# One batch of attention: the product of probabilities and values in plain fp32 instead of hi and lo parts

## The chip, the cores and the metric

The kernel runs on one core of a Trainium2 chip. The metric is the device time of one execution in microseconds (us). A core has a matrix engine (TensorE, PE in the rows; its weight loads are listed apart as PEld), VectorE (DVE), ScalarE (ACT), GpSimd (POOL) and SyncE (SP), which here only issues DMA transfers. Each engine works off its own instructions in their order.

## What is computed

```python
# q, k, v: (4 batches, 12 heads, 448 positions, 64)
q_n, k_n = rmsnorm(q, g_q), rmsnorm(k, g_k)
scores = (q_n @ k_n.T) / sqrt(64)
attn = exp(scores - scores.max(-1)); attn = attn / (attn.sum(-1) + 1e-9)
x = (attn @ v)                       # heads side by side: (1792, 768)
x = relu(x @ w_in)**2 @ w_out        # 768 -> 2048 -> 768
x = ((x @ w1) * (x @ w2)) @ w3 @ w_out2   # 768 -> 1024 -> 1024 -> 768
```

The heads' outputs are gathered to 768 columns and go through two dense blocks. All is fp32 to the caller; the weights arrive as 64-bit numbers.

## The kernel before, in words

**Exact products from rounded parts.** A matmul on tiles of type fp32r rounds its operands. To keep the bits, an operand is written as two fp32r tiles: hi, a rounded copy, and lo, what is left of it (`sub_on`, line 114). A dense product is then three matmuls (lines 262 to 264: hi times hi, hi times lo, lo times hi). ScalarE mostly makes hi (`copy_on`, line 106), GpSimd and VectorE make lo. A weight tile (a "unit", `raw` and `hl` in the rows) goes through a load on SP's queue (line 180), a conversion from 64 bits on ScalarE and GpSimd (lines 194 to 200), a join on VectorE (line 207) and the split.

**Stages.** While the 12 heads of the first batch go through attention, the free slots of TensorE are filled with the product w3 @ w_out2 (`gen_w3o`, 384 matmuls of 384 columns). While the heads of a later batch do so, the dense blocks of the batch before are the filling (`gen_moe`); the last batch's blocks end the kernel. `fill(n)` puts n matmuls of the filling at six places of each head's iteration.

**A head** (loop over `h`, two iterations deep). Scores in two halves of two row chunks each (`stage_qk`, lines 524 to 527: matmuls `sc<-kt,qh` and `sc<-kt,ql`, then the maximum on VectorE), the exponentials on ScalarE (`stage_exp`, line 543, tile `p`), one iteration later the transposes of `p` (`stage_t`, line 570: for each of four key chunks `kc` four transposes into one PSUM tile `pt`), and the product with the values (`stage_v`, line 622: `kv<-ptr,vhl`). The scores have two PSUM tiles, so the next two chunks of scores wait for the exponentials of the last two. Before the change a transposed chunk leaves PSUM twice: ScalarE copies hi, VectorE subtracts lo. The fourth chunk has 64 keys; its hi and lo lie one above the other in one tile (`pte`), so the product is seven matmuls of 448 columns, on weights `vhl` that hold the hi and lo parts of the values side by side (`v_prep`: a copy on VectorE, a subtraction on GpSimd in this batch). Its result has two halves, which ScalarE (tile `vt`) and VectorE (line 630) add up into `xf`. Every second head the row sums (`rsw`) are transposed (line 611) and multiplied in (line 636).

**Order.** The code above is the priority only. A scheduler of the framework sets the order of each engine's instructions from the dependences and its own idea of durations, and hands buffers of a pool to tiles as they come free.

**SP's queue** takes loads and stores in one order. A load whose buffer is not free holds up all that stand behind it. The value tile `v` has two buffers.

Of the kernel before, what the change touches and what calls it, by code (L numbers as in the profile page):

```python
# [8 lines left out]
F32 = mybir.dt.float32  # L9
# [20 lines left out]
def attention_moe_kernel(  # L30
# [15 lines left out]
    nc = tc.nc  # L46
    B, P, H, C, D = q_nat.shape
    S = P * C
# [10 lines left out]
    KCS = ((0, 128), (128, 128), (256, 128), (384, 64))  # L59
# [27 lines left out]
    t2 = ctx.enter_context(tc.tile_pool(name="t2", bufs=2))  # L87
    t1 = ctx.enter_context(tc.tile_pool(name="t1", bufs=1))
    t3 = ctx.enter_context(tc.tile_pool(name="t3", bufs=3))
# [4 lines left out]
    ps_kv = ctx.enter_context(tc.tile_pool(name="ps_kv", bufs=1, space=bass.MemoryType.PSUM))  # L94
# [9 lines left out]
    def copy_on(eng, out, in_):  # L104
        if eng == "a":
            nc.scalar.activation(out=out, in_=in_, func=AF.Copy)  # L106
        elif eng == "g":
            nc.gpsimd.tensor_scalar(out=out, in0=in_, scalar1=1.0, scalar2=1.0, op0=ALU.mult, op1=ALU.mult)
        else:
            nc.vector.tensor_copy(out=out, in_=in_)  # L110

    def sub_on(eng, out, in0, in1):
        e = nc.vector if eng == "v" else nc.gpsimd
        e.tensor_tensor(out=out, in0=in0, in1=in1, op=ALU.subtract)  # L114
# [273 lines left out]
    heads = {}  # L388
# [173 lines left out]
    def stage_t(h, kc):  # L562
        if not (0 <= h < NH):
            return
        d = heads[h]
        k0, kn = KCS[kc]
        ps = ps_pt.tile([128, 512], F32, name="pt", tag="pt")
        to, one = (ps.bitcast(F32R), ident_r) if h >= H else (ps, ident)
        for c in range(C):
            nc.tensor.transpose(to[:kn, c * P:(c + 1) * P], d["p"][c][:, k0:k0 + kn], one)  # L570
        if kn == 128:
            t = t3.tile([128, 2, S], F32R, name="ptr", tag="ptr", bufs=3)
            hi, lo = t[:, 0, :], t[:, 1, :]
            d["pt"][kc] = [hi, lo]
        else:
            t = t1.tile([128, S], F32R, name="pte", tag="pte")
            hi, lo = t[:kn, :], t[kn:, :]
            d["pt"][kc] = [t]
        copy_on("a", hi, ps[:kn, :S])
        d["lo"].append((lo, ps[:kn, :S], hi.bitcast(F32)))  # L580
# [9 lines left out]
    def v_prep(h):  # L590
        if not (0 <= h < NH):
            return
        v = vs.pop(h)
        t = t2.tile([128, C, 2, D], F32R, name="vhl", tag="vhl")
        i = h % 2
        copy_on("v", t[:, :, i, :], v)
        sub_on(VLO_ENG[h // H], t[:, :, 1 - i, :], v, t[:, :, i, :].bitcast(F32))
        heads[h]["v"] = t

    xf = {}  # L600
# [13 lines left out]
    def stage_v(h):  # L614
        if not (0 <= h < NH):
            return
        d = heads.pop(h)
        vt = d["v"].rearrange("p c a d -> p c (a d)")
        ps = ps_kv.tile([128, 512], F32, name="kv", tag="kv")
        ops = [(vt[:, kc, :], m) for kc in range(4) for m in d["pt"][kc]]  # L620
        for n, (w, m) in enumerate(ops):
            nc.tensor.matmul(ps[:, :S], w, m, start=(n == 0), stop=(n == len(ops) - 1))  # L622
        i = h % 2
        r0, r1 = i * D, (1 - i) * D
        if i == 0:
            xf[0] = t2.tile([128, S], F32, name="xf", tag="xf")
        x = xf[0]
        tmp = t1.tile([128, S], F32, name="vt", tag="vt")
        copy_on("a", tmp[r0:r0 + D, :], ps[r1:r1 + D, :S])
        nc.vector.tensor_tensor(out=x[r0:r0 + D, :], in0=ps[r0:r0 + D, :S], in1=tmp[r0:r0 + D, :], op=ALU.add)  # L630
# [45 lines left out]
    for h in range(NH + 1):  # L676
# [8 lines left out]
        if h % H != 1:  # L685
            stage_x(h - 2)
        stage_t(h - 1, 0)
        stage_t(h - 1, 1)
        fill(n)
        stage_lo(h - 1)  # L690
        if h < NH:
            v_prep(h)
        fill(n)
        stage_k(h + 1)
        stage_t(h - 1, 2)
        stage_t(h - 1, 3)
        fill(n)
# [3 lines left out]
        stage_exp(h, 1)  # L701
        fill(n)
        stage_v(h - 1)
        if h % GH == 1:
            group_prep(h // GH + 1)
# [62 lines left out]
```

## Time and profile before

| | |
|---|---|
| median of 3 runs | 1241.29 us (1238.86 to 1243.09) |
| profiled execution, its own time | 1239.56 us |
| span of its trace | 1237.8 us |
| TensorE busy | 1166.3 us, 94% of the span |
| VectorE, ScalarE, GpSimd busy | 57%, 59%, 63% |
| granted TensorE clock, mean | 0.986 |

Shares over the whole span mix stages with different limits, so the rows below go by stretches. In a timeline a row is one or several instructions: start, time from the start of the first to the end of the last, engine, line, operation, tiles, and in brackets the idle time of the engine ahead of it with what ended it. A matmul's listed duration holds its latency: the next one starts while it drains, so the cost of a matmul in a stream is the distance from start to start.

### The profile page before, as it was taken

How to read it: one execution, taken by the hardware profiler on the slowest of the kernel's cores; microseconds unless marked ns; L12 is line 12 of the kernel's file. 1: busy time of each engine (PE TensorE's matmuls, PEld its weight loads, DVE VectorE, ACT ScalarE, POOL GpSimd, SP SyncE). 2: the span in 40 equal slices, each digit the busy share in tenths (PEclk: the TensorE clock that was granted, in tenths of full speed). 3: DMA queues.
4: the chain of work that ended last, by engine and by line, in shares of the span. 5: the costliest groups of instructions: out<-in, count | busy, mean ns of one | idle time of the engine just before them, and what ended most of it. 6: DMA issues, size and time to landing. Idle time of an engine off the chain costs nothing.

```text
span 1237.8 us, 18914 instructions
## 1 busy us (share of the span) xinstructions
PE 1166.3 (94%) x6192; PEld 1054.4 (85%) x6192; DVE 710.7 (57%) x1314; ACT 727.7 (59%) x1553; POOL 784.9 (63%) x772
## 2 busy tenths in 40 slices
PE   3799999898898999999999999999999999999998
PEld 1588887787787888998998998999999999999998
DVE  6699888878888685546567555655664421012110
ACT  5888867667746655655645655656545554443342
POOL 5875434565776756765776664756766556678673
PEclk9899999999999999999999999999999999999999
DMA  6774547787888866455445455454444443433342
GB/s 214 242 227 131 159 140 218 254 272 249 280 259 257 257 192 194 132 155 147 148 127 154 140 155 161 143 154 121 141 138 120 135 136 112 113 109 105 105 120 93
DMA packets 111347, 207.63 MB, mean 168 GB/s; under 512 B 12208, under 2 KB 66704, under 8 KB 111248
## 3 DMA queue, kind: packets, MB, share of 16 engines
q1 hardware_dynamic: 107792, 200.92, 53.8%
q10 hardware_dynamic: 3456, 5.51, 1.2%
q8 instruction: 49, 0.80, 0.3%
q14 instruction: 50, 0.41, 0.1%
HBM read 149.95 MB, written 27.53 MB: 143 GB/s over the span
## 4 chain that ended last, share of the span: by engine, by line
PE 59%; DMA 4%; DVE 4%; ACT 2%; POOL 1%; issue 1%; ACTq 0%; SPq 0%; POOLq 0%; DVEq 0%
PE mm L262 17%; PE mm L264 17%; PE mm L263 17%; PE kv L622 3%; PE pt L570 2%; DMA pw<-p 2%; PE sc L525 1%; PE sc L524 1%; DMA raw<-w 1%; POOL hl L114 1%; ACT p L543 1%; DMA kn<-k_nat 1%; PE kv L508 1%; DVE nb L526 1%; DVE raw L207 0%
## 5 line engine op out<-in xcount | busy, mean ns | idle before, releaser
L114 POOL TENSOR_TENSOR hl<-raw,hl 128x384 fp32r<-128x384 f32 (+1 forms) x383 | 447.0, 1171 | 254.5 <-ACT hl L106 250.9
L106 ACT ACTIVATE hl<-raw 128x384 fp32r<-128x384 f32 (+1 forms) x416 | 233.8, 564 | 146.8 <-PE mm L264 82.0
L262 PE MATMUL mm<-x,hl 128*128 128x448 f32 (+1 forms) x832 | 311.3, 374 | 4.4 <-ACT x L106 1.8
L263 PE MATMUL mm<-x,hl 128*128 128x448 f32 (+1 forms) x832 | 307.2, 369 | 8.1 <-POOL x L114 8.1
L264 PE MATMUL mm<-x,hl 128*128 128x448 f32 (+1 forms) x832 | 306.4, 368 | 3.7 <-DVE hl L114 3.3
L262 PE MATMUL mm<-act,hl 128*128 128x448 f32 (+1 forms) x640 | 238.3, 372 | 0.0
L263 PE MATMUL mm<-act,hl 128*128 128x448 f32 (+1 forms) x640 | 235.7, 368 | 2.3 <-POOL act L114 2.3
L264 PE MATMUL mm<-act,hl 128*128 128x448 f32 (+1 forms) x640 | 235.0, 367 | 0.6 <-POOL hl L114 0.6
L543 ACT ACTIVATE p<-sc,nb,rr 112x448 f32<-112x448 f32 x192 | 137.4, 720 | 82.4 <-DVE nb L527 82.0
L263 PEld LDWEIGHTS mm<-x,hl 128*128 128x128 f32 x832 | 158.5, 190 | 21.9 <-POOL x L114 9.7
L262 PEld LDWEIGHTS mm<-x,hl 128*128 128x128 f32 x832 | 158.4, 190 | 19.6 <-ACT x L106 3.5
L264 PEld LDWEIGHTS mm<-x,hl 128*128 128x128 f32 x832 | 158.6, 191 | 18.3 <-DVE hl L114 4.0
L526 DVE TENSOR_REDUCE nb<-sc 112x1 f32<-112x448 f32 x192 | 113.2, 616 | 34.5 <-PE sc L525 33.0
L263 PEld LDWEIGHTS mm<-act,hl 128*128 128x128 f32 x640 | 122.0, 191 | 12.8 <-POOL act L114 3.6
L200 POOL TENSOR_SCALAR raw<-raw 128x384 uint32<-128x384 uint16 (+1 forms) x110 | 86.3, 785 | 73.3 <-DMA raw<-w_in 25.8
L264 PEld LDWEIGHTS mm<-act,hl 128*128 128x128 f32 x640 | 121.9, 190 | 10.9 <-POOL hl L114 1.3
L262 PEld LDWEIGHTS mm<-act,hl 128*128 128x128 f32 x640 | 122.2, 191 | 9.7 <-ACT act L106 0.2
L114 DVE TENSOR_TENSOR ptr<-pt,ptr 128x448 fp32r<-128x448 f32 x144 | 87.0, 619 | 71.7 <-ACT ptr L106 71.3
L207 DVE SCALAR_TENSOR_TENSOR raw<-raw 128x384 uint32<-128x384 uint32 (+1 forms) x120 | 86.8, 727 | 40.3 <-POOL hl L114 27.2
L114 POOL TENSOR_TENSOR act<-gf,act 128x448 fp32r<-128x448 f32 x80 | 97.8, 1223 | 9.5 <-ACT act L106 5.0
L194 ACT ACTIVATE raw<-raw 128x384 f32<-128x384 f32 (+1 forms) x120 | 70.7, 596 | 52.2 <-DMA raw<-w 19.6
L334 DVE TENSOR_TENSOR gf<-mm,r 128x448 f32<-128x448 f32 x64 | 39.8, 622 | 97.7 <-ACT r L330 97.3
(82 smaller groups left out, 1588.6 us busy)
## 6 DMA issues: line engine op xcount, KB each, us to landing
pw<-p SPq DMA_DIRECT2D x72, 392.0 KB, 4.2
raw<-f_in SPq DMA_DIRECT2D x96, 192.0 KB, 2.4
raw<-f_out SPq DMA_DIRECT2D x72, 256.0 KB, 2.7
raw<-f SPq DMA_DIRECT2D x96, 192.0 KB, 2.4
raw<-w_in SPq DMA_DIRECT2D x32, 384.0 KB, 4.4
raw<-w_out SPq DMA_DIRECT2D x24, 512.0 KB, 6.2
raw<-w SPq DMA_DIRECT2D x32, 384.0 KB, 4.9
raw<-w3o SPq DMA_DIRECT2D x48, 256.0 KB, 2.8
```

The source lines that it names most:

```text
L106: nc.scalar.activation(out=out, in_=in_, func=AF.Copy)
L114: e.tensor_tensor(out=out, in0=in0, in1=in1, op=ALU.subtract)
L194: nc.scalar.activation(out=hi, in_=hi, func=AF.Prelu, scale=2.0**-112, alpha=-(2.0**32))
L200: nc.gpsimd.tensor_scalar(out=t[:, :n, 0], in0=low, scalar1=2.0**-13, scalar2=2.0**-14 - 0.5, op0=ALU.mult, op1=ALU.add)
L207: nc.vector.scalar_tensor_tensor(out=f[:, :n].bitcast(U32), in0=t[:, :n, 1], scalar=3, in1=t[:, :n, 0], op0=ALU.logical_shift_left, op1=AL ...
L262: nc.tensor.matmul(ps, w[:, 0, wk, :], x[0], start=(i == 0), stop=False)
L263: nc.tensor.matmul(ps, w[:, 0, wk, :], x[1], start=False, stop=False)
L264: nc.tensor.matmul(ps, w[:, 1, wk, :], x[0], start=False, stop=(i == last))
L334: nc.vector.tensor_tensor(out=gf, in0=ps, in1=r, op=ALU.mult)
L526: nc.vector.tensor_reduce(out=nb[:, j:j + 1], in_=o[j], axis=AX.X, op=ALU.max, negate=True)
L543: nc.scalar.activation(out=p, in_=o[j], func=AF.Exp, scale=d["rq"][:, c:c + 1], bias=nb[:, j:j + 1], accum_out=sm[:, i, c:c + 1],)
L622: nc.tensor.matmul(ps[:, :S], w, m, start=(n == 0), stop=(n == len(ops) - 1))
```

## The change

In batch 0 only (`h < H`): a transposed chunk leaves PSUM in one plain fp32 copy, on ScalarE for the even chunks and on VectorE for the odd ones; two chunks share a `ptr` tile (so a head takes two of the three buffers, where it took all three and the `pte` tile). The values are used as loaded, without `vhl`. The product is four plain fp32 matmuls into 64 rows, and ScalarE copies the result to its half of `xf`. The transposes and all of batches 1 to 3 stay.

```diff
@@ stage_t
+        if h < H:
+            if kc % 2 == 0:
+                d["pw"] = t3.tile([128, 2, S], F32, name="ptr", tag="ptr", bufs=3)
+            t = d["pw"][:kn, kc % 2, :]
+            d["pt"][kc] = [t]
+            copy_on("av"[kc % 2], t, ps[:kn, :S])
+            return
@@ v_prep
+        if h < H:
+            heads[h]["v"] = v
+            return
@@ stage_v
+        i = h % 2
+        r0, r1 = i * D, (1 - i) * D
+        if i == 0:
+            xf[0] = t2.tile([128, S], F32, name="xf", tag="xf")
+        x = xf[0]
+        if h < H:
+            ps = ps_kv.tile([128, 512], F32, name="kv", tag="kv")
+            for kc, (_, kn) in enumerate(KCS):
+                nc.tensor.matmul(ps[:D, :S], d["v"][:kn, kc, :], d["pt"][kc][0], start=(kc == 0), stop=(kc == 3))
+            copy_on("a", x[r0:r0 + D, :], ps[:D, :S])
+            return
```

The line numbers behind `stage_t` grow: the product in batch 0 is line 636, the transposes of the row sums line 621.

The scheduler places the work of the first stage anew; behind the first heads of batch 1 the order of every engine is as before. On TensorE, in the middle of the first stage, before the change, from the fourth head's product on (`kv<-ptr,vhl`; then filling `mm`, scores `sc`, transposes `pt`):

```order
L622 MATMUL kv<-ptr,vhl 128x448 x6
L622 MATMUL kv<-pte,vhl 128x448
L262 MATMUL mm<-act,hl 128x384
L263 MATMUL mm<-act,hl 128x384
L264 MATMUL mm<-act,hl 128x384
L570 MATMUL pt<-ident,p 128x112 x4
L262 MATMUL mm<-act,hl 128x384
L524 MATMUL sc<-kt,qh 112x448
L525 MATMUL sc<-kt,ql 112x448
```

The same place after the change, from the same head's product on:

```order
L636 MATMUL kv<-ptr,v 64x448 x4
L524 MATMUL sc<-kt,qh 112x448
L525 MATMUL sc<-kt,ql 112x448
L524 MATMUL sc<-kt,qh 112x448
L525 MATMUL sc<-kt,ql 112x448
L262 MATMUL mm<-act,hl 128x384
L263 MATMUL mm<-act,hl 128x384
L264 MATMUL mm<-act,hl 128x384
L621 MATMUL kv<-ident,rsw 128x112 x4
L570 MATMUL pt<-ident,p 128x112 x8
```

The scores now stand right behind the product, and the filling and the transposes that stood between them come later.

On SP's queue, before the change, around the load of the fourth head's values (the third head's stands 15 rows ahead), at the end of the w_out2 units (`wo`) and the start of the w3 units (`w3t`), with the semaphores that a row waits on (`PE_49` is TensorE's):

```order
L180 DMA raw_405<-wo 128x768 [waits DMAHW4_49,DVE_49]
L422 DMA v<-v_in 128x256 [waits DMAHW2_49]
L180 DMA raw_420<-w3t 128x1024 [waits DMAHW5_49,DVE_49]
L180 DMA raw_455<-w3t 128x1024 [waits DMAHW6_49,DVE_49]
L180 DMA raw_467<-w3t 128x1024 [waits DMAHW7_49,DVE_49]
L180 DMA raw_496<-w3t 128x1024 [waits DMAHW1_49,DVE_49]
```

And after it, around the load of the third head's values:

```order
L180 DMA raw_417<-w3t 128x1024 [waits DMAHW4_49,DVE_49]
L180 DMA raw_452<-w3t 128x1024 [waits DMAHW5_49,DVE_49]
L180 DMA raw_464<-w3t 128x1024 [waits DMAHW6_49,DVE_49]
L180 DMA raw_492<-w3t 128x1024 [waits DMAHW0_49,DVE_49]
L422 DMA v<-v_in 128x256 [waits PE_49]
L180 DMA raw_504<-w3t 128x1024 [waits DMAHW1_49,DVE_49]
L180 DMA raw_516<-w3t 128x1024 [waits DMAHW7_49,DMAHW2_49,DVE_49]
```

The load of the third head's values now waits for TensorE, since its buffer comes free with the first head's product and no longer with `v_prep`, and weight loads stand behind it.

## Rows read from the trace of the kernel before

**Rows 1.** The page, busy time and share of the span: TensorE and VectorE.
```profile
span 1237.8 us, 18914 instructions
...
PE 1166.3 (94%) x6192; PEld 1054.4 (85%) x6192; DVE 710.7 (57%) x1314; ACT 727.7 (59%) x1553; POOL 784.9 (63%) x772
```

**Rows 2.** Busy time by stretch; stretches cut at the products of heads.
```profile
core 0: us, PE busy (x) PEld busy (x) DVE busy (x) ACT busy (x) POOL busy (x), PEclk, DMA share, GB/s
...
38.00:85.31 47.31, 39.15 (x190) 33.12 (x191) 39.12 (x68) 38.11 (x83) 37.14 (x39) 0.86 0.74 227
85.31:187.90 102.59, 96.17 (x597) 87.78 (x596) 89.55 (x193) 84.34 (x186) 47.32 (x62) 1.00 0.52 157
187.90:212.00 24.10, 21.06 (x108) 18.35 (x108) 20.97 (x42) 16.64 (x37) 11.02 (x13) 0.93 0.69 196
```

**Rows 3.** Waits of TensorE, 85.31 to 187.90: total us, times, longest.
```profile
PE sc L524 <- ACT p L543: 5.2, 4, 1.6
PE kv L611 <- DVE xf L630: 0.6, 1, 0.6
```

**Rows 4.** TensorE's timeline around one head's product.
```profile
107.99 1.40 PE L622 MATMUL kv<-ptr,vhl 128*128 128x448 f32 x6
109.22 0.37 PE L622 MATMUL kv<-pte,vhl 128*128 128x448 f32 x1
109.43 0.34 PE L262 MATMUL mm<-x,hl 128*128 128x384 f32 x1
...
111.53 0.46 PE L524 MATMUL sc<-kt,qh 128*112 128x448 f32 x1 [1.59 <-ACT p L543]
```

**Rows 5.** TensorE's timeline: eight plain fp32 transposes and the next matmul.
```profile
161.07 0.96 PE L570 MATMUL pt<-ident,p 112*128 112x112 f32 x8
161.81 0.42 PE L262 MATMUL mm<-act,hl 128*128 128x384 f32 x1
```

**Rows 6.** VectorE's groups, 85.31 to 187.90: busy us, mean ns, idle before.
```profile
L114 DVE TENSOR_TENSOR ptr<-pt,ptr 128x448 fp32r<-128x448 f32 x28 | 17.0, 615 | 2.5 <-ACT ptr L106 2.3
...
L114 DVE TENSOR_TENSOR pte<-pt,pte 64x448 fp32r<-64x448 f32 x9 | 5.6, 618 | 0.3
L630 DVE TENSOR_TENSOR xf<-kv,vt 64x448 f32<-64x448 f32 x9 | 5.5, 608 | 0.1
...
L110 DVE CAST vhl<-v 128x256 fp32r<-128x256 f32 x9 | 2.6, 285 | 0.0
```

**Rows 7.** Groups of ScalarE and GpSimd in the same stretch.
```profile
L106 ACT ACTIVATE ptr<-pt 128x448 fp32r<-128x448 f32 x28 | 14.7, 546 | 3.9 <-PE pt L570 3.9
...
L114 POOL TENSOR_TENSOR vhl<-v,vhl 128x256 fp32r<-128x256 f32 x8 | 6.3, 782 | 15.8 <-DVE vhl L110 15.8
```

**Rows 8.** Waits of TensorE, 38 to 85.31.
```profile
PE pt L570 <- DVE nt L432: 2.7, 1, 2.7
PE mm L262 <- ACT hl L106: 0.9, 1, 0.9
...
PE mm L264 <- POOL hl L114: 0.5, 1, 0.5
```

**Rows 9.** Busy time in two short stretches; columns as in rows 2.
```profile
62.00:70.00 8.00, 8.00 (x49) 7.53 (x48) 8.00 (x11) 7.62 (x15) 7.67 (x6) 1.00 0.83 225
70.00:78.00 8.00, 5.28 (x27) 4.60 (x26) 7.80 (x20) 5.24 (x13) 4.11 (x6) 0.83 0.85 236
```

**Rows 10.** Waits of TensorE, 187.9 to 212.
```profile
PE pt L570 <- DMA pw<-p: 2.2, 1, 2.2
PE sc L524 <- ACT p L543: 0.8, 1, 0.8
```

**Rows 11.** Timelines: SP's issues of w3 units; the end of the first head's product.
```profile
49.55 12.56 SPq L180 DMA_DIRECT2D raw<-w3t  x7
...
56.51 0.36 PE L622 MATMUL kv<-pte,vhl 128*128 128x448 f32 x1
```

More of the change, by code (lines that the diff above doesn't have):

```diff
@@ L622, in stage_v @@
             nc.tensor.matmul(ps[:, :S], w, m, start=(n == 0), stop=(n == len(ops) - 1))
[L623 to L627, printed above, removed]
         tmp = t1.tile([128, S], F32, name="vt", tag="vt")
```

## The prediction

> **What bounds the kernel now.** I read the page first, then the stretches, then in each stretch what TensorE waits for. On the page TensorE is busy 94% of the span and no other engine over 63% [rows 1]. The change touches only the 12 heads of batch 0, which lie in the first 188 us, so the whole span says little; the stretches say more. From the third head's product (85.31) to the last one's (187.90) nine heads take 102.59 us, 11.40 us each, with the clock at 1.00, the full level of 2.4 GHz; TensorE is busy 96.17 of them, VectorE 89.55 and ScalarE 84.34 [rows 2]. TensorE thus sets the pace there with 6.4 us of gaps, and of these 5.2 us are one wait, four times: the next scores wait until ScalarE's exponentials have freed their PSUM tile [rows 3]. That wait stands where the reader sees it in rows 4: right behind a head's product TensorE finds only two filling matmuls ahead of scores whose tiles aren't free, and idles 1.59 us. From 38 to 85.31, with the first two heads, it is another matter: TensorE is busy 39.15 of 47.31 us at a mean clock of 0.86, and VectorE, ScalarE and GpSimd between 37 and 39 us [rows 2]; there the supply of weight tiles and VectorE's row of work set the pace as much as TensorE.
>
> **What the product costs.** Six of a head's seven matmuls and the start of the seventh lie from 107.99 to 109.22, so one takes 1.23 / 6 = 0.205 us, and the seven end in the next matmul's start at 109.43: 1.44 us a head [rows 4]. The four new matmuls have as many columns (448), so a pass of one costs 0.205 us whatever its weights; what the trace doesn't show is how many passes a plain fp32 matmul makes. Lower end: one, as the plain fp32 transposes do, eight of which take 161.81 - 161.07 = 0.74 us, 0.09 us each [rows 5]. But a transpose only moves numbers. Upper end: the full product of two operands of hi and lo parts is four fp32r matmuls; the filling already spends three (lines 262 to 264) and drops lo times lo. The kernel shows why one fp32r pass isn't enough: the copy of the values becomes type fp32r [rows 6], and what that rounding drops is subtracted out as lo. A plain matmul that keeps these bits is nearest to those three or four passes, and as nothing in it drops lo times lo I take four: 4 x 4 x 0.205 = 3.28 us, **1.84 us more a head**. With three it would be 2.46 us, 1.02 more.
>
> The Trainium skill bears on this: "FP8 and Floating Point Precision", section TensorE Precision Notes, says that true fp32 goes through the array in four passes, all four products of high and low parts. No run here shows it yet. By it the sum is the one below; by the three passes that the kernel's rows spell out it would be about 1241 us.
>
> **What the change takes off the other engines.** VectorE loses four subtractions of 0.617 us, the copy of the values (0.285) and the addition (0.608) [rows 6], 3.36 us a head, and gets two copies out of PSUM that the trace doesn't show. Bounds: 0.285 us, the copy from SBUF of half as many elements, and 0.617; by the row that reads PSUM (0.608) I take 0.61, so VectorE has 2.1 us less a head, 19 of its 89.55 us. ScalarE loses two of four copies of 0.546 us; its copy of the result stays, with another target. GpSimd loses 0.78 us [rows 7]. None of this is on the path by itself, since TensorE paces the heads; it counts where TensorE waits. The transposes keep their number, and one group of eight costs no less than pieces of it.
>
> **The sum**, against the profiled execution's 1239.56 us (1.73 below the median of 1241.29):
> - Nine heads: 9 x 1.84 = +16.6. The wait for the exponentials goes: the product stands between the scores of one head and the next [rows 4], it is longer by 1.84 us and the longest such wait was 1.6, and both engines of that chain are lighter: -5.2. The 0.6 us for VectorE's addition goes with the addition [rows 3]. Together +10.8.
> - Last head and the change of stage: +1.84, less the 0.8 us wait behind it. The 2.2 us wait for a transfer of batch 1's probabilities stays [rows 10], as that chain starts at the same exponentials. Together +1.0.
> - First two heads: +3.7. Between 62 and 78 VectorE is busy 15.8 of 16 us [rows 9], and in it TensorE waits 2.7 us for VectorE, which has a row of small operations (`nt`) ahead of a subtraction out of PSUM [rows 8]; with 2.1 us less a head on VectorE I let all of it go. After the pause the clock fell: 0.83 over 70 to 78, so 17% of 8 us, 1.4 us, lost at the lower level of 1.2 GHz [rows 9]; it goes with the pause. Waits for weight parts, 0.9 and 0.5 [rows 8], are covered by the longer first product. Together 3.7 - 5.5 = -1.8.
> - SP's queue: the third head's values are loaded only after the first head's product, with w3 loads behind them. Four w3 loads stand ahead in the new order, and at 12.56 / 7 = 1.8 us each from 49.55 they are out at 56.7; the product ended at 56.9 [rows 11]. So the load waits little beyond its turn: 0, and up to 3.3 us (a whole product) if that comes late.
>
> Sum: 10.8 + 1.0 - 1.8 = +10.0, **1249.6 us**, 0.8% over its own time. From batch 1 on nothing is changed but the start.
>
> **Rivals.**
> *Nothing is given back.* The waits move instead of going: the loads on SP come late, the w3 units with them, and TensorE waits for weight parts where it now waits for exponentials. For it: in the first 85 us weight parts are waited for already [rows 8]. Against: behind 85 us no such wait is in the list [rows 3]. Price: 12 x 1.84 = 22.1, 1261.7 us.
> *A cheaper product, faster.* If a plain matmul makes two passes, a head's product costs 1.64 us, 0.2 more, +2.4 in all, and the relief of the first two heads and the addition remains, -6.1: 1236 us. With one pass, -7.4 - 6.1: 1226 us. The relief of 12.1 us in all (5.2 + 0.6 + 0.8 + 5.5) is used up at 12.1 / 12 = 1.0 us a head, that is at three passes; below that it is no slower. For it: the one-pass transposes [rows 5]. Against: three fp32r matmuls for one product.
> The Trainium skill has a rule that points this way: "Perfetto Trace Analysis", section Engine Utilization, halves TensorE's output rate for what it calls FP32_LOW_HIGH. Read as the price of the whole matmul, that is the two passes.
> *The early stretch shrinks far more, no change.* It isn't TensorE that sets it: 39.15 us at clock 0.86 of 47.31. Without the lost clock (0.14 x 47.31 = 6.6) and with 3.7 for the products its work is 36.2 us, so up to 11 us could go; from 8 us on (in place of 1.8 net) the total is +3.8 or less, 1243 us. Against: ScalarE and GpSimd are nearly as busy there [rows 2] and lose little.
>
> **Numbers.** My forecast 0.60, by itself 1245 to 1256 (three and a half passes, to half the waits kept); nothing given back 0.15; cheaper product 0.13; early stretch 0.12. About 0.3%, 3.7 us, is what a measurement of this kernel can tell from no change. Slower: 0.57 of mine and the first rival's 0.15; same: 0.03 of mine, 0.02 of the second (near three passes) and 0.11 of the third; the rest, 0.12, is faster. The range 1238 to 1260 leaves out the cheap product and the end of the first rival.
>
> **What would show it.** The product in batch 0 from its first start to the next matmul: 3.28 us, or 2.46, 1.64, 0.82. A head from product to product about 12.6 us. The wait of scores for exponentials gone from the nine heads. VectorE's busy share there down from 87% to about 62%. No long gap before the second head's product, and the clock near 1.00 at 70 to 78. Behind the first heads of batch 1 the same distances as now. It is wrong if the product takes under 2.5 us, or if TensorE waits anew, for weight parts or a value load.

## The result, and the profile after

The changed kernel takes 1253.88 us (median of four runs, 1249.66 to 1254.32), the kernel before on the same chip 1241.83 (four runs): a ratio of 1.0093 between the means, 95% interval 1.0064 to 1.0121. It is slower, as forecast. The profiled execution took 1249.66 us, 10.1 more than that of before, which was the predicted sum; but it is the fastest of the four runs, the other three lie 4 us above it, and by medians the loss is 12.

The page's first rows: span, and busy time of each engine.

```profile
span 1247.8 us, 18820 instructions
...
PE 1189.6 (95%) x6204; PEld 1047.7 (84%) x6204; DVE 683.8 (55%) x1266; ACT 716.2 (57%) x1529; POOL 771.2 (62%) x760
```

Beside [rows 1] TensorE has 23 us more and every other engine less: the work moved onto the engine that sets the pace. The stretches, cut at the same products as in [rows 2] (columns as there), with the two short ones of [rows 9] behind them:

```profile
38.00:83.74 45.74, 41.87 (x189) 30.02 (x189) 32.70 (x56) 35.23 (x76) 34.43 (x37) 0.89 0.75 248
83.74:197.49 113.75, 112.14 (x606) 84.44 (x605) 71.52 (x157) 75.08 (x164) 39.24 (x53) 1.00 0.46 130
197.49:222.00 24.51, 23.34 (x117) 18.61 (x118) 17.64 (x37) 15.60 (x36) 11.09 (x14) 1.00 0.67 191
...
62.00:70.00 8.00, 8.00 (x54) 7.39 (x53) 7.86 (x13) 7.99 (x17) 6.93 (x6) 1.00 0.92 300
70.00:78.00 8.00, 8.00 (x41) 5.03 (x39) 7.32 (x19) 7.00 (x16) 4.98 (x8) 1.00 0.80 268
```

The nine heads take 113.75 us in place of 102.59, 12.64 us each, and TensorE's gaps there fell from 6.4 us to 113.75 - 112.14 = 1.6. The third head's product comes 1.57 us earlier (83.74, not 85.31). Behind the last product 1247.8 - 197.49 = 1050.3 us are left, where there were 1049.9: 0.4 more. 11.2 - 1.6 + 0.4 is the 10.0 us between the spans. VectorE's share in the heads is 71.52 of 113.75, 63%, and the clock over 70 to 78 is back at 1.00 with no gap.

What TensorE waits for in the nine heads (total us, times, longest):

```profile
PE kv L621 <- ACT xf L106: 0.9, 1, 0.9
PE kv L636 <- ACT kt L106: 0.3, 1, 0.3
PE pt L570 <- DVE ptr L110: 0.3, 1, 0.3
```

The 5.2 us for the exponentials [rows 3] are gone. TensorE's timeline around one product:

```profile
135.08 3.36 PE L636 MATMUL kv<-ptr,v 128*64 128x448 f32 x8
138.38 0.46 PE L524 MATMUL sc<-kt,qh 128*112 128x448 f32 x1
```

From start to start 138.38 - 135.08 = 3.30 us, where [rows 4] gave 1.44. The program has four matmuls here and the trace eight, of 0.41 us each. The copies of full transposed chunks out of PSUM in the nine heads, VectorE's then ScalarE's (busy us, mean ns); VectorE's other copies, of the fourth chunk's 64 rows, are listed with 610 ns:

```profile
L110 DVE COPY ptr<-pt 128x448 f32<-128x448 f32 x9 | 5.6, 622 | 1.5 <-PE pt L570 1.3
...
L106 ACT ACTIVATE ptr<-pt 128x448 f32<-128x448 f32 x18 | 9.7, 538 | 0.0
```

### The profile page after: what moved, and what is told of

Read it like the earlier page. It is cut to its first block, busy times and chain, and to the rows that moved or that the text cites. A ratio compares the mean times of both kernels' runs of the same rounds, so it can differ in the third digit from the quotient of the medians.

```text
span 1247.8 us, 18820 instructions
## 1 busy us (share of the span) xinstructions
PE 1189.6 (95%) x6204; PEld 1047.7 (84%) x6204; DVE 683.8 (55%) x1266; ACT 716.2 (57%) x1529; POOL 771.2 (62%) x760
## 4 chain that ended last, share of the span: by engine, by line
PE 56%; DMA 5%; DVE 3%; POOL 3%; issue 2%; ACT 2%; SPq 0%; POOLq 0%; ACTq 0%; DVEq 0%
PE mm L262 16%; PE mm L264 16%; PE mm L263 16%; PE kv L643 3%; PE pt L570 2%; DMA raw<-w 2%; POOL hl L114 2%; DMA kn<-k_nat 1%; PE sc L525 1%; PE sc L524 1%; DMA pw<-p 1%; PE kv L508 0%; ACT p L543 0%; POOL raw L200 0%; DVE nb L526 0%
## 5 line engine op out<-in xcount | busy, mean ns | idle before, releaser
L200 POOL TENSOR_SCALAR raw<-raw 128x384 uint32<-128x384 uint16 (+1 forms) x110 | 81.3, 739 | 83.5 <-DMA raw<-w_in 36.6
L114 DVE TENSOR_TENSOR ptr<-pt,ptr 128x448 fp32r<-128x448 f32 x108 | 64.9, 619 | 68.6 <-ACT ptr L106 68.6
```

The lines of the kernel that those rows point to most:

```text
L200: nc.gpsimd.tensor_scalar(out=t[:, :n, 0], in0=low, scalar1=2.0**-13, scalar2=2.0**-14 - 0.5, op0=ALU.mult, op1=ALU.add)
```

## The experiments

The number behind each time is its ratio to the kernel before on the same chip, with the 95% interval; the groups of runs were made on different chips, on which the kernel before took 1237.40 to 1240.67 us, so versions are compared by these ratios. Stretches and waits are those of one profiled execution each.

### Is the price the product's?

**The product twice** (e8_double), on the changed kernel; all 12 products of batch 0 are made twice, the second four matmuls writing over the result of the first:

```diff
-            for kc, (_, kn) in enumerate(KCS):
+            for kc, (_, kn) in 2 * list(enumerate(KCS)):
```

> The change with the product made twice (eight plain fp32 matmuls a head, the second four over the first). Theory (in the heads of the first batch TensorE's work counts fully once the wait is gone): 3.30 us more a head from product to product, 15.9 us, and 37 to 40 us in all, about 1290 us. Rival (there is still slack on TensorE that takes part of it): under 33 us in all.

1290.72 us (4 runs), 1.0425 [1.0406, 1.0444]. TensorE's timeline:

```profile
140.71 6.65 PE L636 MATMUL kv<-ptr,v 128*64 128x448 f32 x16
147.29 0.45 PE L524 MATMUL sc<-kt,qh 128*112 128x448 f32 x1
```

A doubled product is 6.58 us, 16 times 0.41. From the third head's product (91.50) to the last one's (236.88) the heads take 16.15 us, 3.51 more than with one product, and the profiled executions differ by 1290.94 - 1249.66 = 41.3 us, 3.4 a head, a little over the 37 to 40 of the theory. What is added to the product (6.58 - 3.30 = 3.28 us) is paid in full here, and a little more.

**All copies on one engine** (e5_copies_act, and e6_copies_dve with `"v"`), on the changed kernel:

```diff
-            copy_on("av"[kc % 2], t, ps[:kn, :S])
+            copy_on("a", t, ps[:kn, :S])
```

> The change with all copies of transposed chunks on ScalarE, none on VectorE. Theory (TensorE sets the pace of the heads, the other engines have room): within 2 us of the changed kernel, 12.6 us a head. Rival (ScalarE's row of work, with 1.1 us more a head, holds back the exponentials and so the scores): the wait of scores for exponentials is back, 13 us a head, 4 us or more over the changed kernel.

> The change with all copies of transposed chunks on VectorE, none on ScalarE. Theory: within 2 us of the changed kernel behind the second head; in the first two heads, where VectorE is busy nearly all the time, up to 2 us slower. Rival (VectorE's work of 1.2 us more a head sets the pace): 13 us a head, 4 us or more over the changed kernel.

On ScalarE alone: 1250.86 us (4 runs), 1.0099 [1.0079, 1.0119] beside 1.0093 for the changed kernel, 12.66 us a head: nothing changed. On VectorE alone: 1256.05 (4 runs), 1.0142 [1.0124, 1.0160]; the later heads keep their pace (12.50 us), but the third head's product starts at 89.81, 6 us later. The nine heads of both, ScalarE alone first, then TensorE's longest wait ahead of the third head's product with VectorE alone, and VectorE's timeline in that wait:

```profile
85.45:199.41 113.96, 111.58 (x605) 84.71 (x604) 63.09 (x143) 83.05 (x182) 39.47 (x53) 1.00 0.46 135
89.81:202.34 112.53, 111.31 (x605) 84.85 (x604) 78.53 (x177) 67.22 (x145) 39.24 (x52) 1.00 0.46 135
...
PE pt L570 <- DVE ptr L110: 5.6, 1, 5.6
...
69.27 0.69 DVE L207 SCALAR_TENSOR_TENSOR raw<-raw 128x512 uint32<-128x512 uint32 x1 [3.75 <-POOL raw L200]
```

So in the nine heads the split of the copies isn't what costs: TensorE's gaps are 2.4 and 1.2 us. In the first two heads TensorE still runs into VectorE, though not for the copies' own length: ahead of them VectorE stands for 3.75 us in a join that waits for GpSimd's conversion of a weight unit.

**Four value buffers** (e7_v_bufs), so that the third head's values needn't wait for the first product:

```diff
-        t = t2.tile([128, C, D], F32, name="v", tag="v")
+        t = t2.tile([128, C, D], F32, name="v", tag="v", bufs=4)
```

> The change with four buffers for the values in place of two, so that their loads no longer wait on SP's queue for the product. Theory (that wait costs nothing): within 2 us of the changed kernel, the third head's product at 83 to 84.5 us. Rival (weight loads stand behind the waiting load and TensorE waits for them): 2 to 5 us faster, the gain ahead of the third head's product.

1254.59 us (4 runs), 1.0142 [1.0115, 1.0168], 12.59 us a head: no gain, if anything slower than the changed kernel's 1.0093. The changed kernel's SP queue shows the late load, with weight loads behind it:

```profile
47.96 5.43 SPq L180 DMA_DIRECT2D raw<-w3t  x4
58.17 0.33 SPq L422 DMA_DIRECT2D v<-v_in  x1
58.59 2.88 SPq L180 DMA_DIRECT2D raw<-w3t  x3
```

SP does stand still there (6.9 us in two waits for TensorE's product, from 20 to 100 us; before the change it was 6.0 us in two waits for GpSimd's part of `v_prep`). With four buffers this load is out at 49.36 and the waits for the product are gone. Yet the third head's product starts at 85.77, 2.0 us later than in the changed kernel and outside the 83 to 84.5 of the theory, so the late load is not what costs; the edit brought another order with it.

### Why did the wait for the exponentials go?

The prediction gave two reasons: a longer product between the scores, and lighter side engines. Each was tried alone.

**The relief without the long product** (e1_one_pass): the changed kernel, with the probabilities and the values rounded to fp32r, so one pass each.

```diff
-                d["pw"] = t3.tile([128, 2, S], F32, name="ptr", tag="ptr", bufs=3)
+                d["pw"] = t3.tile([128, 2, S], F32R, name="ptr", tag="ptr", bufs=3)
...
-            heads[h]["v"] = v
+            t = t2.tile([128, C, D], F32R, name="vh", tag="vh")
+            copy_on("v", t, v)
+            heads[h]["v"] = t
```

> The change with the product as four fp32r matmuls on rounded probabilities and values (the lo parts are left out, so the product is less exact; a rounding copy of the values of 0.28 us on VectorE comes back). Theory (the product's length on TensorE is the cost): the product falls from 3.30 to 0.83 us a head, TensorE's work of a head to about 10.0 us; part of the wait for the exponentials comes back, since the product is now shorter than before the change, so 10.4 to 11.2 us a head and 1222 to 1233 us. Rival (the new order or the transfers of the values cost the time): 12 us a head or more, over 1243 us.

1240.26 us (10 runs), 0.9993 [0.9977, 1.0009]: no faster than before, and a miss. The product is short (TensorE's timeline, and the busy times from 122 to 127):

```profile
117.13 1.10 PE L638 MATMUL kv<-ptr,vh 128*64 128x448 f32 x4
118.16 0.44 PE L262 MATMUL mm<-act,hl 128*128 128x384 f32 x1
...
121.95 0.71 PE L524 MATMUL sc<-kt,qh 128*112 128x448 f32 x1 [2.82 <-ACT p L543]
...
122.84 0.52 PE L263 MATMUL mm<-act,hl 128*128 128x384 f32 x1
123.16 0.52 PE L264 MATMUL mm<-act,hl 128*128 128x384 f32 x1
...
122.00:127.00 5.00, 5.00 (x20) 4.65 (x21) 2.62 (x7) 2.74 (x7) 0.54 (x1) 0.50 0.26 74
```

It takes 118.16 - 117.13 = 1.03 us, 2.27 less than in plain fp32, which is 20.4 us in nine heads. They became only 8.7 us shorter than in the changed kernel:

```profile
83.31:188.32 105.01, 97.98 (x569) 86.02 (x568) 74.82 (x167) 74.91 (x165) 41.99 (x54) 0.93 0.51 148
```

Two things took the other 11.7. TensorE's gaps are 105.01 - 97.98 = 7.0 us, 5.4 more than in the changed kernel; and its busy time fell by 14.2 instead of 20.4, with the mean granted clock at 0.93. The rows above show the link: behind the pause of 2.82 us the 384-column matmuls follow each other at 0.32 us (122.84 to 123.16), at the lower level (the last row: a granted clock of 0.50, that is 1.2 GHz), where they take 0.17 ahead of the pause (118.62 to 118.79). The pause is a chain over three engines. VectorE's timeline, and below it one row of GpSimd's:

```profile
118.63 0.69 DVE L207 SCALAR_TENSOR_TENSOR raw<-raw 128x512 uint32<-128x512 uint32 x1 [3.33 <-POOL hl L114]
119.24 1.15 DVE L526 TENSOR_REDUCE nb<-sc 112x1 f32<-112x448 f32 x2
...
117.32 1.28 POOL L114 TENSOR_TENSOR hl<-raw,hl 128x512 fp32r<-128x512 f32 x1
```

VectorE's next instruction is the join of a weight unit, which waits 3.33 us for GpSimd's split of an older unit to free a buffer. The maxima of the scores stand behind it and start only at 119.24; the exponentials wait for them, and the next scores for the exponentials. VectorE isn't short of time (74.82 of 105.01), only held up in its order.

**The long product without the relief** (e2_long_old): the kernel before, with nine repeats of its fp32r matmuls added to each product of batch 0, 16 passes in all; the seven matmuls of before come last and write over what the nine gave.

```diff
+        if h < H:
+            more = (ops + ops)[:9]
+            for n, (w, m) in enumerate(more):
+                nc.tensor.matmul(ps[:, :S], w, m, start=(n == 0), stop=(n == len(more) - 1))
```

> The kernel before, with nine extra fp32r passes ahead of the seven in batch 0 (written over by the seven): a product as long as the changed one, 3.28 us, with all the old work of hi and lo parts left on VectorE, ScalarE and GpSimd. Theory (the longer product itself covers the wait for the exponentials): the wait gone from the nine heads, about 12.6 us a head, first two heads 2 us slower than before, 1251 to 1256 us. Rival (the lighter VectorE and ScalarE took the wait away): the wait stays at over half of its 5.2 us, 13.0 us a head or more, 1258 to 1263 us.

1263.29 us (4 runs), 1.0176 [1.0152, 1.0201], and 13.53 us a head. The stretch of nine heads, then TensorE's waits in it:

```profile
86.53:208.31 121.78, 113.94 (x677) 102.33 (x677) 90.74 (x194) 83.30 (x182) 44.14 (x60) 1.00 0.43 126
...
PE pt L570 <- DVE ptr L114: 3.4, 3, 2.0
PE sc L524 <- ACT p L543: 3.1, 4, 1.1
PE kv L611 <- DVE xf L634: 0.9, 1, 0.9
```

The long product takes 2.1 of the 5.2 us off the wait for the exponentials, and 3.4 us of new waits for VectorE's subtraction take their place: gaps of 7.8 us. The rival was right, with a time at the very end of its range. In VectorE's order the joins wait here too, 8.8 us in all. But e5 has 12.9 us of such waits in its nine heads, and ScalarE as busy as here (83.05 us), with gaps of only 2.4: neither of the two makes the gaps by itself. What e5 has less of is VectorE's work, 63.09 us where e2 has 90.74.

**Filling moved between product and scores** (e4_fill_shift), on the kernel before: in batch 0 the third of the six pieces of filling goes ahead of the product's place, so that more stands ahead of the scores.

```diff
-        fill(n)
+        if h >= H:
+            fill(n)
...
-        fill(n)
+        fill(n if h >= H else 2 * n)
```

> The kernel before; in batch 0 the third of the six pieces of filling moves from between the two halves of a head's scores to ahead of the product, so that about 0.9 us more of TensorE's work lies between one head's scores and the next's. Theory (the wait for the exponentials goes with any work of TensorE at this place): at least half of the 5.2 us in nine heads go, 10.9 to 11.2 us a head, 1235 to 1239 us. Rival (the wait moves to the place from which the filling was taken): 11.4 us a head, 1240 to 1243 us.

1239.94 us (12 runs), 0.9992 [0.9978, 1.0006]: no change, as the rival had it. The nine heads, and TensorE's waits in them:

```profile
86.15:189.88 103.73, 97.98 (x596) 87.14 (x596) 93.80 (x194) 84.93 (x186) 48.67 (x63) 1.00 0.53 157
...
PE pt L570 <- DVE ptr L114: 1.4, 2, 0.9
PE sc L524 <- ACT p L543: 1.3, 3, 0.7
PE kv L508 <- DVE rs L554: 1.1, 1, 1.1
PE kv L611 <- DVE xf L630: 1.0, 2, 0.6
PE kv L622 <- DVE ptr L114: 0.5, 1, 0.5
```

The wait for the exponentials falls from 5.2 to 1.3 us, and waits for VectorE, busy 90% of the stretch, fill the hole. That speaks for reading the 5.2 us of [rows 3] as the place where VectorE's lateness showed; that the order of instructions has a say in this wait as well, the next run shows.

### The first two heads

**The change for two heads only** (e3_two_heads): `h < 2` for `h < H` in the three places.

```diff
-        if h < H:
+        if h < 2:
```

> The change for the first two heads only. Theory (there TensorE waits for others, so the longer product is hidden and the relief counts): the third head's product starts 1 to 2 us earlier than before (at 83.5 to 84.5 us against 85.3) and the rest is as before: 1236 to 1240 us. Rival (what the first two heads gain is given back in the heads after them): the last head's product no earlier than before, 1240 to 1243 us.

1247.66 us (8 runs), 1.0053 [1.0035, 1.0071], a miss: the early gain was to stay, but the third head's product starts at 91.52, 6.2 us later than before. TensorE's row ahead of it, and VectorE's at the same time:

```profile
86.70 0.86 PE L570 MATMUL pt<-ident,p 112*128 112x112 f32 x4 [3.98 <-DVE ptr L114]
...
84.51 1.60 DVE L207 SCALAR_TENSOR_TENSOR raw<-raw 128x512 uint32<-128x512 uint32 x1 [3.56 <-POOL hl L114]
86.03 1.14 DVE L114 TENSOR_TENSOR ptr<-pt,ptr 128x448 fp32r<-128x448 f32 x2
```

It is the chain of e1: the new order has a join, waiting for a buffer, ahead of the third head's subtractions. And this is only a part of the loss. The nine heads behind it have their old code, yet take 106.63 us in place of 102.59, and the scores wait 9.0 us for exponentials where it was 5.2:

```profile
91.52:198.15 106.63, 97.44 (x597) 89.18 (x596) 88.62 (x188) 81.42 (x180) 46.28 (x58) 0.98 0.47 133
...
PE sc L524 <- ACT p L543: 9.0, 6, 1.9
```

So the same code, ordered anew, can cost 4 us more in these heads. The join ahead of the subtractions led to a theory that could be tried: with a fifth buffer for joined weights the join has no split to wait for.

### A fifth buffer for the joins

All four have one edit:

```diff
-    rawp = ctx.enter_context(tc.tile_pool(name="raw", bufs=4))
+    rawp = ctx.enter_context(tc.tile_pool(name="raw", bufs=5))
```

**On e3** (e12_two_heads_raw5).

> The change for the first two heads only, with five instead of four buffers for joined weight tiles. New theory: the 4.0 us in which TensorE waits for VectorE ahead of the third head's product (VectorE waits 3.6 us with a join for GpSimd there) go, the third head's product starts at 84 to 88 us instead of 91.5, 1240 to 1245 us. Rival (the pause there has another cause): still at 90 us or later, 1246 us or more.

1240.42 us (12 runs), 1.0013 [0.9996, 1.0029], 0.4 points or 5 us under e3. The third head's product starts at 86.49, not 91.52, and of TensorE's wait ahead of it is left:

```profile
PE pt L570 <- DVE ptr L114: 0.9, 1, 0.9
```

The theory holds for what the join cost. The loss in the nine heads stays: they take 107.05 us, with 9.8 us of waits for exponentials. Beside the kernel before with the same five buffers (e10 below, 1236.20 us on the same chip) this version is still 4.2 us slower.

**On e1** (e9_one_pass_raw5).

> The one-pass product of before, with five instead of four buffers for joined weight tiles. New theory (what held the one-pass heads was VectorE's own order: a join of a weight tile waits for a buffer that GpSimd's subtraction frees, and the maxima of the scores stand behind the join): the waits of VectorE's joins for GpSimd in the nine heads fall from 10.5 us to under 4, the wait of the scores for exponentials with them, 10.2 to 11.0 us a head, 1225 to 1234 us. Rival (the chain from scores to exponentials is too long for the shorter product whatever the joins do): 11.4 us a head or more, 1237 us or more.

1234.85 us (10 runs), 0.9962 [0.9945, 0.9979], by the ratios some 4 us under e1, and between the two ranges: the theory's ended at 1234, and its other two figures fail by more. VectorE's waits for the join halve, from 10.5 us (e1, five times), where under 4 were expected, to:

```profile
DVE raw L207 <- POOL hl L114: 5.3, 3, 2.9
```

The heads take 11.25 us in place of 11.67, not 10.2 to 11.0. TensorE's gaps are still 101.28 - 94.56 = 6.7 us, and one head of 15.85 us stays (16.22 in e1), from 113.11 on. In it the chain of e1 stands again, a join that waits for GpSimd, then the maxima, the exponentials, and TensorE:

```profile
114.32 0.56 DVE L207 SCALAR_TENSOR_TENSOR raw<-raw 128x384 uint32<-128x384 uint32 x1 [2.88 <-POOL hl L114]
...
117.50 0.71 PE L524 MATMUL sc<-kt,qh 128*112 128x448 f32 x1 [2.39 <-ACT p L543]
```

The granted clock over this head is 0.78. So the fifth buffer takes away a part of these waits and not all.

**On the kernel with the long product and the old work** (e11_long_old_raw5).

> The long product with the old work of hi and lo parts, with five instead of four buffers for joined weight tiles. If the joins' wait alone kept the gaps (8.8 us of VectorE's waits), the gaps of TensorE in the nine heads fall from 7.8 to under 4 us, 12.6 to 13.1 us a head, 1254 to 1259 us: then the longer product does cover the wait without the relief of VectorE. Rival (VectorE's extra 2.1 us a head keeps them): the gaps stay at 6 us or more, 13.3 us a head or more, 1260 us or more.

1261.56 us (4 runs), 1.0180 [1.0157, 1.0203], 13.50 us a head, gaps 121.51 - 113.74 = 7.8 us: nothing changed there. But VectorE's wait for the join stayed as well (8.0 us, 8.8 in e2), so this run by itself doesn't tell whether the gaps of e2 come from that wait or from VectorE's larger work; e5, with longer join waits and small gaps, speaks for the work.

**On the kernel before** (e10_before_raw5).

> The kernel before with five instead of four buffers for joined weight tiles. New theory: in its nine heads the joins wait for GpSimd only 1.7 us, so little is to be had there; 0 to 4 us faster than before in all, from the first two heads and the start of batch 1. Rival (the order that the scheduler then finds decides more than the buffer): anything from 6 us faster to 6 us slower, with a change in the first two heads.

1236.20 us (12 runs), 0.9978 [0.9964, 0.9993]. The first two heads are as before (the third head's product starts at 85.34), against the theory, and so are the nine heads (103.17 us); the gain lies behind them, 1232.0 - 188.51 = 1043.5 us in place of 1049.9. A part of that is run to run, since the profiled execution lies 2.4 us under its own median. It is the only version with the full computation that beats both kernels clear of noise, by 0.2% over before.

## Why the prediction was right

The mechanism held where most of the time is, in the price of the product and in the nine heads. That the profiled execution hit the sum to 0.1 us was luck: the four runs of the changed kernel spread over 4.7 us, and their median lies 4.3 us above the sum, inside the stated range.

**The product's price**: four passes, 3.28 us, measured 3.30, and 3.5 us a head when it is doubled. The Trainium skill's four passes ("FP8 and Floating Point Precision", TensorE Precision Notes) agree: 3.30 us is 16.1 times the 0.205 of [rows 4]. The rate that the Trainium skill halves for FP32_LOW_HIGH ("Perfetto Trace Analysis", Engine Utilization), the ground of the rival with two passes, fits each of the eight matmuls in the trace (0.41 us), but a matmul of the program is two of these.

Two smaller steps of that part don't come out. That the plain transposes make one pass isn't shown by [rows 5]: at 0.205 us for 448 columns one pass over 112 columns would be 0.05 us, not 0.09. And with three passes the sum would be 1249.6 - 12 x 0.82 = 1239.8 us on its own base, not about 1241. The forecast uses neither.

**Nine heads**: +10.8 predicted, +11.2 measured. The size was right, a reason for it was too simple. The step said that the wait for the exponentials goes as "it is longer by 1.84 us and the longest such wait was 1.6, and both engines of that chain are lighter". The gaps of TensorE in the nine heads, span less busy time, each from the stretch of one profiled execution:

| | VectorE's old work | lighter engines |
|---|---|---|
| short product | 6.4 us (before), 6.8 (e10), 5.8 (e4), 9.2 (e3), 10.4 (e12) | 7.0 (e1), 6.7 (e9) |
| long product | 7.8 (e2), 7.8 (e11) | 1.6 (the change), 2.4 (e5), 1.2 (e6), 1.3 (e7) |

Neither part takes the gaps away alone; only both together do. Comparing the product's extra with the longest wait was no proof, since in e2 that wait shrank and others came up. Each version has an order of its own from the scheduler. Within a cell the gaps differ by up to 4.6 us, but the four versions of the last cell stay at 2.4 us or less (e8, with the product doubled, has 3.8) and none of the other cells comes under 5.8, which speaks against an accident of one order. Of the two engines that the prediction called lighter, ScalarE wasn't needed: in e5 it is as busy as in e2, and the wait for the exponentials stays away. What the right column has besides lighter work isn't separated from it: GpSimd's part of `v_prep` gone, and two `ptr` buffers for a head in place of all three.

**First two heads**: -1.8 predicted, -1.6 measured. TensorE's gaps from 38 us to the third head's product fell from 8.2 us (47.31 - 39.15) to 3.9 (45.74 - 41.87), 4.3 less where 4.1 were taken off. The three waits that were to go did go, but that the sums agree is partly luck. The prediction left out the largest wait of the stretch, 3.0 us for a lo part (`x`) that GpSimd makes out of a weight unit, which fell by 2 us (before, then after):

```profile
PE mm L263 <- POOL x L114: 3.0, 2, 2.1
...
PE mm L263 <- POOL x L114: 1.0, 1, 1.0
PE mm L262 <- ACT x L106: 0.8, 1, 0.8
PE pt L570 <- ACT ptr L106: 0.8, 1, 0.8
```

The last two rows are waits that weren't there before, and they take most of that back. TensorE's busy time rose by 2.7, where 3.7 for products less 1.4 for the clock makes 2.3. And this gain is no property of VectorE's lower load: with the same change in these heads the third head's product starts at 85.77 in e7, 86.49 in e12 and 91.52 in e3, where the kernel before has 85.31. Of all versions with the full computation only the changed kernel is earlier. Here the scheduler's order was a kind one, which the prediction hadn't looked at, so the -1.8 was luck.

**Last head and change of stage**: +1.0 predicted, +0.4 measured. The wait for batch 1's probabilities [rows 10], which was to stay, fell from 2.2 to 0.3 us:

```profile
PE kv L621 <- ACT xf L106: 0.8, 1, 0.8
PE pt L570 <- DMA pw<-p: 0.3, 1, 0.3
```

So that step was wrong. A new wait of 0.8 stands beside it. The 0.4 itself says little: behind the last head the work is the same in every run, and with four weight buffers the time from the last product's start on was 1049 to 1053 us in the profiled executions.

**SP's queue**: 0 predicted, and e7 shows no gain when the load is early. The wait itself was mis-sized: the weight loads ahead were out at 47.96 + 5.43 = 53.4, and the value load left at 58.17, 4.8 us later, where 0.2 and at most 3.3 were worked out.

**The rivals**: against "nothing is given back" (1261.7) stands the vanished wait, though e2, which keeps the old work, lands there (1263.29). "A cheaper product" falls with the 3.30 us. "The early stretch shrinks far more" needed 8 us, and the stretch shrank by 1.6.

**Open**: where the other three runs of the changed kernel spent 4 us more than the profiled one; what share the joins' waits have in e2's gaps beside VectorE's larger work; and what the `ptr` buffers and GpSimd's relief add to the last cell of the table.

## What to carry to other kernels

Price a plain fp32 product as four passes, as measured here: on an engine that sets the pace, trading VectorE's and GpSimd's work for those passes pays only what TensorE waited for, here 12 of 22 us between the profiled executions. Before a wait is counted as gain, ask whether it is the place or the cause: moving work in front of it (e4), or lengthening what lies ahead (e2), only showed the next one. On an in-order engine look for an instruction that waits for a buffer ahead of one on the critical chain; one more buffer there gave some 5 us (e3 to e12, by the ratios) where such a join held up TensorE. And count with the scheduler: an edit in the first two heads moved the nine distances behind them by 4 us in all, so a gain of one stretch in one order is not yet a gain of the change.

## What the runs showed of the hardware that was not expected

- One plain fp32 matmul appears as two pairs of a weight load and a matmul, each of 0.41 us for 448 columns, also where it has only 64 rows of weights; a load of 64 columns took 0.136 us.
- A pause of TensorE of 2.8 us was paid more than once: behind it the granted clock was 0.50 for at least 5 us (e1, 122 to 127: 0.32 us from one 384-column matmul to the next, not 0.17). In e1's nine heads the busy time came out 6.2 us above what the shorter product alone would give, about as much as the gaps (7.0).
- The copy of 128x448 from PSUM is listed with 0.62 us on VectorE and 0.54 on ScalarE, the first as long as the subtraction that it replaced (0.615, [rows 6]).
